# The exact-maxima path of a fused attention and FFN block as a second pass behind the last store, and two jobs of the FFN moved

## The chip, the cores and the metric

One core of a Trainium2 chip runs the whole kernel. The metric is the device time in microseconds (us), taken as the median of repeated runs; a profiled execution beside them gives the trace. PE is the matrix engine (PEld its weight loads), ACT the scalar engine, DVE the vector engine, POOL GpSimd, SP the engine that issues the DMAs.

## The reference

A pre-norm transformer block without biases, in float32, on 2048 tokens of width 576. There are 32 query heads of 18, one shared key head and one shared value head, and a bilinear FFN of width 4608.

```python
h  = x + attention(layernorm(x))           # q = x@wq, k = x@wk, v = x@wv, softmax(q k^T / sqrt(18)) v @ wo
h2 = h + ((layernorm(h) @ w_gate) * (layernorm(h) @ w_up)) @ w_down
```

## The kernel before

**Blocks and pairs.** The tokens are worked on in four blocks of 512. The unit of attention is a *pair* (`pair`, `scores`, `values`): one tile of 128 keys against 512 queries of two heads. PE multiplies (L498) into a PSUM tile `s`, of which there are two, ACT takes the exponential of 128x1024 elements into `P` (L499), and PE later multiplies `P` with the values into `acc` (L503), which is done by `flush`. Eight groups of four heads, 16 key tiles and two pairs for each make 256 pairs per block, 1024 in all. Queries of block 0 run by themselves at the start, first beside the projection of the queries, then alone (`steps`). All other pairs are put between the matmuls of the FFN of earlier blocks.

**The guard.** The softmax subtracts an upper bound of the maxima, worked out from the absolute queries, in place of the maxima. `flag` compares the largest bound with a limit, and `guard` (L384 to L395) branches on the result: with these inputs the bound is below the limit and the branch body is skipped. The body computes the exact maxima (`exact_maxima`) and repeats the seven groups of block 0 that are done by then (`again`, `chunk_of`). It stands in the middle of the attention of block 0, after pair 224. Every engine loads the flag into a register (L387) and branches (L388). A hint for the branch stands at the start of the program for PE, ACT, DVE and SP.

**Projection.** When a group of heads is done, `normalise` and `normal_heads` (L528 to L560) divide by the row sum (`rc`, L544 to L547), transpose, and regroup the rows by DMAs into `ob` (L560). A chunk of `ob` is split into a high and a low part (`chunk`, L563) and multiplied with a chunk of `wo` (`project`, L630). For blocks 1 to 3 `wo`'s chunks are loaded one after the other into one buffer `wor` (`load_wo`, L588), called from `chunk`, and split by POOL and DVE into `wos` (`split_wo`, L88 and L89) in the round after. These jobs wait in a list, and `run_aux` takes one job of it in each *round*; there are two rounds per FFN step (after matmul step 12, and at the end).

**FFN.** Each block has 36 steps of 128 hidden units. A step multiplies `X` with the gate and up weights (L836, 27 pairs of matmuls into `pg` and `pu`, for which there are two PSUM tiles in all), ACT copies one result to `g` (L859), DVE multiplies the other with it to `hf` (L863). Two steps together are multiplied with their part of `w_down` by a scheme of seven products (`down`, L796, 14 stages over three PSUM banks). The results are added to the residual by DVE (L799) or by ACT and POOL (L803, L804). This is done at the end of the next even step. The seven weight combinations are made once, in the FFN of block 0: `right_sums` (L913 to L924) makes three sums on POOL (L915), called at matmul step 16 of the even step; `right` makes the high part on POOL (L939) and the low part on DVE (L942) in the odd step, at matmul steps 7, 9 and so on, and stores them (L945) for the later blocks. `raw` (L911) is the load of the next `w_down` part, issued when `right` ends.

**Order.** The order of instructions on every engine is the order of the calls (a manual schedule). Each engine works its own list strictly in that order and waits on semaphores, so an instruction that waits holds up all that stand behind it on its engine.

At a change of block, `spread` transposes the normalised rows (L679) and splits them into `X`; five chunks are transposed in the order 0 to 4 and taken out of PSUM in the order 4, 0, 2.

Of the kernel before, what the change touches and what calls it, by code (L numbers as in the profile page):

```python
# [17 lines left out]
F32 = mybir.dt.float32  # L18
# [7 lines left out]
P = 128  # L26
# [32 lines left out]
class Block:  # L59
# [312 lines left out]
    def flag(self):  # L372

        dve, lp = self.dve, self.lp
        mx1 = lp.tile([H, 1], F32, tag="mx1", bufs=1, name="mx1")
        dve.tensor_reduce(mx1, self.mx[:, 0:self.n_mx], AX.X, ALU.max)
        psx = self.ps_m("psx")
        self.pe.transpose(psx[0:1, 0:H], mx1, self.ident[:H, :H])
        mx2 = lp.tile([1, 1], F32, tag="mx2", bufs=1, name="mx2")
        dve.tensor_reduce(mx2, psx[0:1, 0:H], AX.X, ALU.max)  # L380
        self.above = lp.tile([1, 1], I32, tag="flag", bufs=1, name="flag")
        dve.tensor_scalar(self.above, mx2, GUARD / SCALE, None, ALU.is_gt)

    def guard(self):  # L384

        self.tc.mark_branch_hint_location("guard", "LikelyTaken", [getattr(mybir.EngineType, e) for e in ("PE", "Activation", "DVE", "SP")])
        fv = self.nc.values_load(self.above, min_val=0, max_val=1, skip_runtime_bounds_check_because="a comparison")  # L387
        with self.tc.If(fv > 0, label="guard"):  # L388
# [8 lines left out]
    def again(self, g):  # L397

        q = self.pp.tile([P, 2, TB], F32R, tag="P", name=f"qa{g}")
        self.load_q(q, 0, g)  # L400
        self.load_m(q, 0, g)
        acc = self.ps_a(f"acca{g}")
        for t in range(NT):
            Ps = []
            for pr in range(2):
                s_ = self.ps_s(f"sa{g}_{t}_{pr}")
                p_ = self.pp.tile([P, 2, TB], F32, tag="P", name=f"Pa{g}_{t}_{pr}")
                self.scores(s_, p_, q, t, pr)
                Ps.append(p_)
            self.values(acc, Ps, t)  # L410
            del Ps, p_, s_
        os_ = self.os.get(g)
        if os_ is None:
            os_ = self.pp.tile([P, TB], F32, tag="P", name=f"osa{g}")
        self.dve.transpose(os_, acc)
        if g not in self.os:
            self.normal_heads(0, g, os_)

    def load_q(self, q, b, g):
        for i, o in enumerate((0, 64)):  # L420
# [107 lines left out]
    def normalise(self, b, g, os_):  # L528
        if g == 0:
            self.ob = self.op.tile([P, 5, TB], F32, tag="ob", name=f"ob{b}")  # L530
        self.normal_heads(b, g, os_)
        del self.os[g]
        c = ({1: 0, 3: 1, 5: 2, 6: 3, 7: 4} if b == 0 else {1: 0, 3: 1, 5: 2, 7: 3}).get(g)
        if c is not None:
            self.aux.append((self.round + (LANDING if b == 0 and c < 4 else 0), lambda: self.chunk(b, c), None))

    def normal_heads(self, b, g, os_):


        dve, ob = self.dve, self.ob  # L540
        o = os_.rearrange("p (k c) -> p k c", c=32)
        rc = self.op.tile([P, TB // 32], F32, tag="rc", bufs=2, name=f"rc{b}_{g}")
        if b == 0:
            dve.tensor_scalar(rc, o[:, :, 0], 1e-30, None, ALU.max)  # L544
            dve.reciprocal(rc, rc)
        else:
            dve.reciprocal(rc, o[:, :, 0])  # L547
        dve.tensor_tensor(o[:, :, 1:1 + DH], o[:, :, 1:1 + DH],
                          rc.unsqueeze(2).broadcast_to([P, TB // 32, DH]), ALU.mult)
        turned = ob[:, 4 if b == 0 or g < NG - 1 else 0]  # L550
        dve.transpose(turned, os_)
        if b == 0 and g == NG - 1:
            return
        for j in range(4):
            r, end, m = DH * (4 * g + j), DH * (4 * g + j + 1), rows(b, 0)
            p = 32 * j + 1
            while r < end:
                c, n = r // m, min(end, (r // m + 1) * m) - r
                for q in (r % m, 64 + r % m)[:1 if c < 4 else 2]:
                    self.sp.dma_start(ob[q:q + n, c], turned[p:p + n])  # L560
                r, p = r + n, p + n

    def chunk(self, b, c):  # L563
# [102 lines left out]
    def spread(self, b):  # L666
# [49 lines left out]

    def more_wd(self, b, n):

        if b:
            self.load_wd(self.n_wd + n)  # L720

    def left_first(self, n, hf):
# [93 lines left out]
    def ffn(self, b):  # L816
        pe, act, dve = self.pe, self.act, self.dve
        X, hid, todo = self.X, [], None
        for f in range(NF):
# [11 lines left out]
            for c in range(9):  # L831
                for wk, xk in ((0, 0), (0, 1), (1, 0)):
# [41 lines left out]
            todo = (f // 2,) if k else None  # L874
        if b + 1 < NB:
            both(self.spread(b + 1), self.down(b, *todo))
            self.more_wd(b + 1, WD_BUFS if b == 0 else 4)
            if b + 2 < NB:
                self.load_x(b + 2)
        else:  # L880
# [45 lines left out]
    def right(self, p):  # L926
# [21 lines left out]
        self.src = None  # L948
        self.load_raw(p + 1)

    def run(self):
# [4 lines left out]
        self.wd_list = [(b, p, j) for b in range(1, NB) for p in range(NC) for j in (range(4) if p == NC - 1 else ORDER)]  # L956
        self.n_wd = 0
        self.m_dram = tc.dram_tile([NB, 2, H, TB], F32, name="m_dram")
        self.known, self.n_mx, self.os, self.chunks = [0] * NB, 0, {}, []
        self.h, self.qt, self.normed, self.wr, self.ws, self.wdo, self.wo_r, self.wos = {}, {}, {}, {}, {}, {}, {}, {}  # L960
        self.n_pair, self.half, self.pend, self.aux, self.round = 0, [], [], [], 0
        self.tqs = []
        self.p2, self.p_next, self.wo_from, self.due = None, -1, 10 ** 6, 0.0
        with ExitStack() as st:
            pool = lambda name, bufs, **k: st.enter_context(tc.tile_pool(name=name, bufs=bufs, **k))
            cp, self.lp, self.hp = pool("const", 1), pool("ln", 2), pool("resid", 2)
# [9 lines left out]
            with tc.tile_pool(name="p0q", bufs=1) as self.p0q:  # L976
# [3 lines left out]
                with tc.tile_pool(name="qb", bufs=2) as self.qb:  # L980
# [7 lines left out]
                    while live:  # L988
# [18 lines left out]
            self.cast = self.act.copy  # L1007
            self.load_w(0)
            self.load_w(1)
            self.fill(2.0, 1)  # L1010
            while 0 not in self.normed:
                self.run_aux(1)
                self.fill(1.0, 1)
            self.split_w(0)
            while self.n_pair % 8 != 4:
                self.pair()
                if not self.half:
                    self.flush(len(self.pend) - 1)
            self.flush(len(self.pend))
            self.normal(0)  # L1020
            for _ in range(2):
                self.pair()
            for i, _ in enumerate(self.spread(0)):
                if i % 2 == 0:
                    self.pair()
            self.flush(len(self.pend))
            del self.oT
            self.room()
            self.load_raw(0)
            for b in range(NB):  # L1030
                self.ffn(b)


RATE = 3.0
# [130 lines left out]
```

## Time and profile before

| | us |
|---|---|
| median of 3 runs | 2355.78 |
| the runs | 2352.33, 2355.87, 2355.78 |
| the profiled execution, its time | 2353.41 |
| the profiled execution, its span | 2351.6 |
| PE busy | 2294.3 |
| ACT busy | 1431.7 |
| DVE busy | 1184.3 |
| POOL busy | 673.8 |
| mean granted PE clock | 0.993 of full speed |

The span runs from the first to the last instruction of the trace; the time of that execution is 1.8 us more. Busy time of PE includes the time in which a pipelined matmul runs under the next. Times in the views are counted from the start of the span.

### The profile page before, as it was taken

The numbers are of one execution on the slowest core, as the hardware profiler recorded it, in microseconds if no ns is written. First come the engines' busy times: TensorE is split into PE (matmuls) and PEld (weight loads), VectorE is DVE, ScalarE is ACT, GpSimd is POOL, SyncE is SP. The second block draws the span as 40 slices with busy tenths as digits, with TensorE's granted clock in tenths as the row PEclk, the third lists the DMA queues.
The fourth block names the chain that finished last, engine by engine and source line by source line (L and its number), as shares of the span: only waits on it lengthen the run. The fifth ranks groups of instructions, "written<-read, shape, count | busy, mean of one in ns | idle before, by whom it ended". The sixth has DMA issues, their size and how long they took to land.

```text
span 2351.6 us, 46322 instructions
## 1 busy us (share of the span) xinstructions
PE 2294.3 (98%) x18225; PEld 1611.6 (69%) x18225; DVE 1184.3 (50%) x2151; ACT 1431.7 (61%) x1868; POOL 673.8 (29%) x873
## 2 busy tenths in 40 slices
PE   5999999999999999999999999999999999999999
PEld 4334434677776767777777667766777778888888
DVE  7333334565555556444444445544444476565665
ACT  4788877766676666567676767567676623232322
POOL 3100000455454444222222212312222224343333
PEclk9999999999999999999999999999999999999999
DMA  4222222444333443633433333544333335655443
GB/s 142 69 65 84 71 80 69 148 147 141 128 125 123 139 149 134 201 117 122 127 122 117 121 100 122 153 156 127 112 121 120 113 129 190 197 188 185 168 167 126
DMA packets 127218, 306.52 MB, mean 130 GB/s; under 512 B 15679, under 2 KB 16447, under 8 KB 126999
## 3 DMA queue, kind: packets, MB, share of 16 engines
q1 hardware_dynamic: 126999, 303.54, 39.6%
q8 instruction: 145, 2.38, 0.4%
q14 instruction: 74, 0.61, 0.1%
HBM read 234.00 MB, written 55.67 MB: 123 GB/s over the span
## 4 chain that ended last, share of the span: by engine, by line
PE 79%; issue 3%; DVE 2%; POOL 1%; ACT 1%; DMA 0%; SPq 0%; DVEq 0%; POOLq 0%; ACTq 0%
PE y L796 17%; PE pg L836 14%; PE acc L503 14%; PE gu L836 12%; PE pu L836 9%; PE s L498 9%; PE yo L630 3%; PE y L754 1%; ACT P L499 1%; POOL x L804 0%; POOL ws L88 0%; PE ye L754 0%; DVE hf L863 0%; DMA X<-X 0%; DVE bsb L103 0%
## 5 line engine op out<-in xcount | busy, mean ns | idle before, releaser
L499 ACT ACTIVATE P<-s 128x1024 f32<-128x1024 f32 x1024 | 1025.3, 1027 | 311.8 <-PE s L498 232.4
L836 PE MATMUL pg<-X,ws 64*128 64x512 f32 x2565 | 699.5, 391 | 0.0
L836 PE MATMUL pu<-X,ws 64*128 64x512 f32 x2565 | 699.2, 391 | 0.0
L836 PEld LDWEIGHTS pg<-X,ws 64*128 64x128 f32 x2565 | 476.5, 186 | 56.2 <-DMA wr<-in_wgu_dram 0.8
L836 PEld LDWEIGHTS pu<-X,ws 64*128 64x128 f32 x2565 | 473.9, 186 | 37.1 <-DVE h L631 0.3
L503 PE MATMUL acc<-P,V 128*32 128x512 f32 x4096 | 492.2, 600 | 0.9 <-ACT P L499 0.6
L498 PE MATMUL s<-q,kT 56*128 56x512 f32 x2048 | 439.1, 423 | 7.0 <-ACT P L499 3.9
L796 PEld LDWEIGHTS y<-wdo,room 128*128 128x128 f32 x2856 | 389.3, 189 | 61.7 <-issue 46.9
L796 PE MATMUL y<-wdo,room 128*128 128x288 f32 x2856 | 410.9, 302 | 10.2 <-DVE hf L863 5.2
L803 ACT COPY tmp<-y 128x288 f32<-128x288 f32 x408 | 162.5, 399 | 341.2 <-PE y L796 326.1
L498 PEld LDWEIGHTS s<-q,kT 56*128 56x128 f32 x2048 | 195.9, 185 | 208.6 <-ACT P L499 119.4
L836 PE MATMUL gu<-X,ws 64*128 64x512 f32 x2646 | 308.1, 389 | 0.3 <-DMA X<-X 0.2
L836 PEld LDWEIGHTS gu<-X,ws 64*128 64x128 f32 x2646 | 258.0, 184 | 43.9 <-issue 3.8
L503 PEld LDWEIGHTS acc<-P,V 128*32 128x32 f32 x4096 | 114.8, 109 | 250.3 <-issue 232.5
L804 POOL TENSOR_TENSOR x<-x,tmp 128x288 f32<-128x288 f32 x204 | 159.2, 811 | 411.9 <-ACT tmp L803 410.5
L88 POOL CAST ws<-wr 128x1152 fp32r<-128x1152 f32 x144 | 168.4, 1170 | 322.8 <-PE gu L836 102.4
L804 POOL TENSOR_TENSOR h<-h,tmp 128x288 f32<-128x288 f32 x204 | 159.5, 810 | 327.0 <-ACT tmp L803 326.5
L89 DVE TENSOR_TENSOR ws<-wr,ws 128x1152 fp32r<-128x1152 f32 x144 | 196.7, 1366 | 75.2 <-POOL ws L88 75.2
L863 DVE TENSOR_TENSOR hf<-pu,g 128x512 f32<-128x512 f32 x95 | 65.5, 689 | 258.2 <-ACT g L859 258.1
L799 DVE TENSOR_TENSOR x<-x,y 128x288 f32<-128x288 f32 x272 | 117.1, 452 | 143.4 <-PE y L796 143.4
L799 DVE TENSOR_TENSOR h<-h,y 128x288 f32<-128x288 f32 x272 | 117.2, 453 | 95.4 <-PE y L796 92.6
L89 DVE TENSOR_TENSOR room<-S,room 128x1024 fp32r<-128x1024 f32 x68 | 83.3, 1225 | 152.9 <-ACT room L88 152.9
(170 smaller groups left out, 1716.9 us busy)
## 6 DMA issues: line engine op xcount, KB each, us to landing
wdo<-wd_dram SPq DMA_DIRECT2D x369, 288.0 KB
wr<-in_wgu_dram SPq DMA_DIRECT2D x144, 576.0 KB
wd_dram<-wdo SPq DMA_DIRECT2D x123, 288.0 KB
q<-q_dram SPq DMA_DIRECT2D x64, 216.0 KB
raw<-in_wd_dram SPq DMA_DIRECT2D x36, 288.0 KB
q_dram<-qs SPq DMA_DIRECT2D x16, 504.0 KB
X<-X SPq DMA_DIRECT2D x28, 256.0 KB
x<-in_x_dram SPq DMA_DIRECT2D x16, 288.0 KB
```

What stands on the lines that cost most here:

```text
L88: (copy or self.cast)(hi, src)
L89: self.dve.tensor_tensor(lo, src, f32(hi), ALU.subtract)
L498: self.pe.matmul(s_[:, i], self.kT[o:o + 56, t * P:(t + 1) * P], q[o:o + 56, pr], start=True, stop=True)
L499: self.act.activation(p_, s_, AF.Exp, scale=SCALE)
L503: self.pe.matmul(acc[32 * j:32 * j + 32, :], self.V[:, t, :], Ps[j // 2][:, j % 2, :], start=(t == 0), stop=(t == NT - 1), skip_group_chec ...
L630: pe.matmul(y[:, :HD], m, k, start=(i == 0), stop=(i == len(ms) - 1))
L796: pe.matmul(y[:, :HD], m[:, t * P:(t + 1) * P], k, start=(first and j == 0), stop=(j == 2), skip_group_check=True)
L799: dve.tensor_tensor(hs, hs, y[:, :HD], ALU.add)
L803: act.copy(z, y[:, :HD])
L804: pool.tensor_tensor(hs, hs, z, ALU.add)
L836: pe.matmul(ps, w[o:o + 64, wk, c], X[o:o + 64, xk, c], start=(j == 0), stop=(j == 26))
L863: dve.tensor_tensor(hf, pu, g, ALU.mult)
```

## The change

Five things are edited.

1. The guard moves behind the last store of the whole program. Its body is now a complete second pass: exact maxima, then attention and FFN of all blocks again (`begin(False)`, `blocks`). The hint is dropped. `again` goes, and the list of chunks with it. POOL now has work in the body too. To serve both passes, the code from the load of the first `wo` on is put into `blocks`.
2. With that the pairs of block 0 run on without the flush at pair 224: `load_wo_0` is split over the steps up to pair 228, the flag is worked out in the steps up to pair 236, and the projections of block 0 may begin at pair 240 instead of 236.
3. `right_sums` is called at matmul step 4 of the odd step, no longer at step 16 of the even one.
4. `load_wo` of chunks 0 to 3 is called from `normalise`, ahead of the DMAs of `ob`; chunk 4's stays in `chunk`. `split_wo` waits one round more after the load.
5. `normal_heads` bounds the row sum from below in all blocks, not in block 0 alone (one more DVE instruction on 128x16 per group), and `spread` transposes chunk 4 first in blocks 1 to 3.

```diff
     def guard(self):
-        self.tc.mark_branch_hint_location("guard", "LikelyTaken", [getattr(mybir.EngineType, e) for e in ("PE", "Activation", "DVE", "SP")])
         fv = self.nc.values_load(self.above, min_val=0, max_val=1, skip_runtime_bounds_check_because="a comparison")
         with self.tc.If(fv > 0, label="guard"):
             self.exact_maxima()
-            for g in range(self.n_pair // (2 * NT)):
-                self.again(g)
-            for c in self.chunks:
-                self.chunk_of(0, c)
-            for (b, g), q in self.qt.items():
-                self.load_m(q, b, g)
+            self.begin(False)
+            self.known = [H] * NB
+            self.prefetch_q(0, 0)
+            self.load_x(0)
+            self.load_x(1)
+            self.blocks()
...
     def normalise(self, b, g, os_):
...
+        c = ({1: 0, 3: 1, 5: 2, 6: 3, 7: 4} if b == 0 else {1: 0, 3: 1, 5: 2, 7: 3}).get(g)
+        if b and c is not None:
+            self.load_wo(c)
         self.normal_heads(b, g, os_)
         del self.os[g]
-        c = ({1: 0, 3: 1, 5: 2, 6: 3, 7: 4} if b == 0 else {1: 0, 3: 1, 5: 2, 7: 3}).get(g)
...
-        if b == 0:
-            dve.tensor_scalar(rc, o[:, :, 0], 1e-30, None, ALU.max)
-            dve.reciprocal(rc, rc)
-        else:
-            dve.reciprocal(rc, o[:, :, 0])
+        dve.tensor_scalar(rc, o[:, :, 0], 1e-30, None, ALU.max)
+        dve.reciprocal(rc, rc)
...
     def chunk(self, b, c):
...
-        if b == 0:
-            self.chunks.append(c)
-        else:
+        if b and c == 4:
             self.load_wo(c)
...
-        if self.wo_r and not self.wos and self.wo_round < self.round:
+        if self.wo_r and not self.wos and self.wo_round + 1 < self.round:
...
-        for c, n, t in sorted(tx, key=lambda x: x[0]):
+        for c, n, t in tx:
...
-                    if b == 0 and j == 16 and not k:
-                        self.right_sums(f // 2)
-                        parts = self.right(f // 2)
-                    if b == 0 and k and j > 6 and j % 2:
-                        next(parts, None)
+                    if b == 0 and k and self.first:
+                        if j == 4:
+                            self.right_sums(f // 2)
+                            parts = self.right(f // 2)
+                        elif j > 6 and j % 2:
+                            next(parts, None)
...
+    def blocks(self):
+
+        work = self.load_wo_0()
+        self.steps(lambda: self.n_pair < WO_FROM, work)
+        drain(work)
+        self.wo_from = WO_FROM + 12
+        if self.first:
+            work = self.flag()
+            self.steps(lambda: self.n_pair < WO_FROM + 8, work)
+            drain(work)
+        self.cast = self.dve.tensor_copy
+        self.steps(lambda: self.more(0))
+        self.cast = self.act.copy
...
+        for b in range(NB):
+            self.ffn(b)
...
     def run(self):
...
-            self.flag()
             self.wp, self.hh, self.p2 = pool("w", 2), pool("hid", 4), pool("P2", 1)
-            wo_parts = self.load_wo_0()
-            self.steps(lambda: self.n_pair % (2 * NT), wo_parts)
-            self.flush(len(self.pend))
+            self.blocks()
             self.guard()
-            self.wo_from = self.n_pair + 12
-            self.steps(lambda: self.more(0), wo_parts)
-            drain(wo_parts)
...
+WO_FROM = 228
```

`flag` gets a `yield` after its first instruction, so that its PE transpose comes one step later. The rest of the moved code, from the first load of gate weights to the FFN loop, is the same in `blocks` as it was in `run`.

More of the change, by code (lines that the diff above doesn't have):

```diff
@@ L717, in more_wd @@
     def more_wd(self, b, n):
-        if b:
+        if b or not self.first:
             self.load_wd(self.n_wd + n)
@@ L876, in ffn @@
             both(self.spread(b + 1), self.down(b, *todo))
-            self.more_wd(b + 1, WD_BUFS if b == 0 else 4)
+            self.more_wd(b + 1, WD_BUFS if b == 0 and self.first else 4)
             if b + 2 < NB:
@@ L949, in right, with begin @@
         self.load_raw(p + 1)
+    def begin(self, first):
+        self.first = first
+        self.wd_list = [(b, p, j) for b in range(first, NB) for p in range(NC) for j in (range(4) if p == NC - 1 else ORDER)]
+        self.n_wd = 0
+        self.os, self.h, self.qt, self.normed, self.wr, self.ws, self.wdo, self.wo_r, self.wos = ({} for _ in range(9))
+        self.n_pair, self.half, self.pend, self.aux, self.round = 0, [], [], [], 0
+        self.p_next, self.wo_from, self.due = -1, 10 ** 6, 0.0
+    def blocks(self):
[10 more added lines that the diff above has]
+        self.cast = self.act.copy
+        self.load_w(0)
+        self.load_w(1)
+        self.fill(2.0, 1)
+        while 0 not in self.normed:
+            self.run_aux(1)
+            self.fill(1.0, 1)
+        self.split_w(0)
+        while self.n_pair % 8 != 4:
+            self.pair()
+            if not self.half:
+                self.flush(len(self.pend) - 1)
+        self.flush(len(self.pend))
+        self.normal(0)
+        for _ in range(2):
+            self.pair()
+        for i, _ in enumerate(self.spread(0)):
+            if i % 2 == 0:
+                self.pair()
+        self.flush(len(self.pend))
+        del self.oT
+        self.room()
+        if self.first:
+            self.load_raw(0)
+        else:
+            self.load_wd(WD_BUFS)
+        for b in range(NB):
+            self.ffn(b)
+        del self.A, self.o_hl, self.S, self.tmp, self.X, self.ob, self.mv
     def run(self):
@@ L955, in run @@
         self.wd_dram = tc.dram_tile([NC, P, 7, 2, HD], F32, name="wd_dram")
-        self.wd_list = [(b, p, j) for b in range(1, NB) for p in range(NC) for j in (range(4) if p == NC - 1 else ORDER)]
-        self.n_wd = 0
         self.m_dram = tc.dram_tile([NB, 2, H, TB], F32, name="m_dram")
[L959 to L963, printed above, removed]
+        self.known, self.n_mx = [0] * NB, 0
+        self.tqs, self.p2 = [], None
+        self.begin(True)
         with ExitStack() as st:
@@ L997, in run @@
                         self.flush(len(self.pend) - 1)
-            self.flag()
             self.wp, self.hh, self.p2 = pool("w", 2), pool("hid", 4), pool("P2", 1)
-            wo_parts = self.load_wo_0()
-            self.steps(lambda: self.n_pair % (2 * NT), wo_parts)
-            self.flush(len(self.pend))
+            self.blocks()
             self.guard()
-            self.wo_from = self.n_pair + 12
-            self.steps(lambda: self.more(0), wo_parts)
-            drain(wo_parts)
[L1007 to L1031, printed above, removed]
 RATE = 3.0
```

21 lines of the change are left out of this document (1 added, 20 removed).

## The prediction

> **What bounds the kernel now.** I read the page's busy times first, then PE's rows with an idle time before them, then what ended those waits, then the granted clock of the stretches behind them.
>
> ```profile
> PE 2294.3 (98%) x18225; PEld 1611.6 (69%) x18225; DVE 1184.3 (50%) x2151; ACT 1431.7 (61%) x1868; POOL 673.8 (29%) x873
> ```
>
> PE is busy for 2294.3 of 2351.6 us, so nearly everything beside PE is hidden, and an edit that leaves PE's work alone can gain only where PE stands still (57 us in all) or runs slowly. Behind the start, which the change doesn't touch, two kinds of place stand out. The first is the guard:
>
> ```profile
> 323.24 0.73 PE L498 MATMUL s<-q,kT 56*128 56x512 f32 x4 [2.38 <-SPq L388]
> 315.99 3.77 ACT L499 ACTIVATE P<-s 128x1024 f32<-128x1024 f32 x4 [1.43 <-PE s L498]
> 323.83 3.85 ACT L499 ACTIVATE P<-s 128x1024 f32<-128x1024 f32 x4 [4.07 <-PE s L498]
> 329.25 1.94 ACT L499 ACTIVATE P<-s 128x1024 f32<-128x1024 f32 x2 [1.57 <-PE s L498]
> 332.26 3.77 ACT L499 ACTIVATE P<-s 128x1024 f32<-128x1024 f32 x4 [1.07 <-PE s L498]
> 325.40:332.20 6.80, 6.38 (x28) 1.69 (x26) 2.73 (x5) 4.22 (x5) 0.00 (x0) 0.50 0.35 90
> ```
>
> In these rows come start, duration, engine and line; in brackets the idle time before and what ended it. Here attention runs alone, and ACT sets the pace: 3.77 us for four exponentials, 0.943 us each. At the branch PE waits 2.38 us for SP's branch (L388) and ACT loses 4.07 us. The last row is a stretch of time with each engine's busy time; its third figure from the end is the granted clock of PE: 0.50. The trace shows half speed right behind the stall, and ACT loses 1.57 and 1.07 us more to it.
>
> The second kind is in the FFN, six times:
>
> ```profile
> PE y L796 <- DVE hf L863: 5.2, 4, 3.1
> 878.84 1.54 PE L796 MATMUL y<-wdo,room 128*128 128x288 f32 x5 [3.06 <-DVE hf L863]
> 1393.15 1.13 PE L630 MATMUL yo<-wos,room 128*128 128x288 f32 x5 [1.90 <-DVE h L631]
> 1891.54 1.87 PE L796 MATMUL y<-wdo,room 128*128 128x288 f32 x8 [3.58 <-DVE h L799]
> 870.92 0.43 SPq L588 DMA_DIRECT2D wor<-in_wo_dram  x1
> 876.06 0.67 POOL L88 CAST wos<-wor 128x576 fp32r<-128x576 f32 x1 [15.85 <-DMA wor<-in_wo_dram]
> 876.76 1.33 DVE L89 TENSOR_TENSOR wos<-wor,wos 128x576 fp32r<-128x576 f32 x1 [7.87 <-POOL wos L88]
> POOL wos L88 <- DMA wor<-in_wo_dram: 103.3, 13, 15.8
> ```
>
> The first of these rows is from the view of waits: 5.2 us in 4 waits, the longest 3.1, which is the next row; the other three are near 503, 627 and 752. PE names DVE, but at 876 DVE itself stood idle for 7.87 us: its next instruction, the low part of `wos`, waited for POOL's high part, and that for the load of `wo`, which SP had issued 5.1 us before. The last row, from the view of waits too, says that POOL meets 13 loads like this.
>
> **Part 1, the guard leaves the attention.** From 315.99 to 332.26 ACT does 10 exponentials in 16.27 us; at 0.943 they take 9.43, so 6.84 go. Ahead of it 1.43 us of idle time become the usual 0.2 or so, since the transpose of the flag now comes a step after the reduction it waits for. Together **-8.0**. What is late next is the end of block 0's chain: its projections start 4 pairs later, while the FFN begins at the same pair.
>
> ```profile
> 379.09 0.37 PE L630 MATMUL yo<-wo,oT 128*128 128x288 f32 x1 [0.55 <-ACT oT L88]
> 384.14 0.66 PE L630 MATMUL yo<-wo,oT 128*128 128x288 f32 x3 [0.58 <-DVE x L631]
> 391.30 1.70 POOL L663 COPY xh<-xh 128x64 f32<-128x64 f32 x4 [53.88 <-DVE xh L662]
> 396.69 2.40 PE L679 MATMUL tx<-C,xh 128*128 128x128 f32 x20 [0.95 <-ACT P L499]
> ```
>
> From the last projection (384.80) the normalised rows take until 393.00, 8.2 us; today 10 pairs cover this, 10.9 us of PE; in the new order 7 pairs remain, some 7.7 us and the wait of 0.95. That just holds. Chunk 3's high part moves to ACT, behind exponentials, where chunk 4's already costs 0.55. I charge **+0.7** (0 to 3).
>
> **Part 2, wo's loads.** Chunks 0 to 3 are loaded a round earlier, ahead of `ob`'s DMAs and what follows them in SP's queue.
>
> ```profile
> 857.33 6.73 SPq L560 DMA_DIRECT2D ob<-ob  x9
> 1879.25 6.89 SPq L560 DMA_DIRECT2D ob<-ob  x9
> 1886.18 0.47 SPq L588 DMA_DIRECT2D wor<-in_wo_dram  x1
> ```
>
> At 870.92 the load moves to about 857, at 1886.18 to about 1879: 7 to 13 us earlier, against the 5.1 us to its landing. The split stays in the round that it has now, because the extra round of waiting balances the earlier load; so DVE finds its data there. All six stalls belong to chunks 0 to 3. Their gaps sum to 5.2 + 1.90 + 3.58 = 10.7 us. Three of them are followed by half speed:
>
> ```profile
> 878.30:881.70 3.40, 2.86 (x12) 2.89 (x13) 1.58 (x4) 0.67 (x2) 2.00 (x3) 0.50 0.00 0
> 1393.70:1397.10 3.40, 3.40 (x15) 3.12 (x16) 2.33 (x7) 0.00 (x0) 0.00 (x0) 0.51 0.00 0
> 1892.10:1895.50 3.40, 3.40 (x16) 3.40 (x16) 0.83 (x2) 1.19 (x3) 1.94 (x3) 0.50 0.32 89
> 1885.65 1.35 DVE L89 TENSOR_TENSOR ws<-wr,ws 128x1152 fp32r<-128x1152 f32 x1
> ```
>
> Each 3.4 us at 0.50 loses 1.7, together 5.1. At 1888 a rest stays: `ws` ends at 1887.0, the low part of `wos` (1.33) still stands before the residual adds, so PE resumes near 1888.85 and not at 1887.96: 0.9. Sum **-14.9** (-5 to -16). The Trainium skill's page "TensorE: Matmul & The Clock Gate", section "What's actually happening", says that the clock is halved after about one idle window of 3.4 us; by that rule gaps of 1.90 and 3.06 us would be too short, the 5.1 would not be there, and the sum would end 5.1 us higher. The trace disagrees: 0.51 behind the gap of 1.90. Each load costs SP 0.43 us ahead of `ob`'s DMAs, which are used a round later and have that time.
>
> **Part 3, the right sums.** Three POOL instructions move from a step in which POOL has time to the odd step of block 0, ahead of the casts that feed DVE, with `hf` behind them in DVE's queue, and PE's next step needs the PSUM tile that `hf` reads. Two such steps, without and with a group's normalisation in them:
>
> ```profile
> L915 POOL TENSOR_TENSOR sums<-raw,sums x17: 799/809/1191, 411.8 to 903.5; 128x288 f32<-128x288 f32 x17
> 454.33 0.66 POOL L939 CAST wdo<-raw 128x288 fp32r<-128x288 f32 x1
> 459.36 0.50 PE L498 MATMUL s<-q,kT 56*128 56x512 f32 x2
> 484.57 0.65 POOL L939 CAST wdo<-raw 128x288 fp32r<-128x288 f32 x1
> 485.82 1.39 DVE L942 TENSOR_TENSOR wdo<-raw,wdo 128x288 fp32r<-128x288 f32 x1
> 487.13 0.68 DVE L863 TENSOR_TENSOR hf<-pu,g 128x512 f32<-128x512 f32 x1
> 489.38 0.50 PE L498 MATMUL s<-q,kT 56*128 56x512 f32 x2
> ```
>
> Three sums of 0.81 put POOL's last cast 2.43 us later: 457.4 and 487.65. DVE's last low part then runs beside POOL's next cast, as it does at 485.82, and takes 1.39: 458.8 and 489.05. `hf` ends at 459.5 and 489.75. PE needs its tile 0.33 us after the quoted pair: 459.7 and 489.7. So nothing to 0.1 in the 9 plain steps, 0.1 to 0.4 in the 8 others: 9 x 0.05 + 8 x 0.25 = **+2.5** (0 to 32, below).
>
> **Part 4, the branch at the end.** SP is last there.
>
> ```profile
> 2345.13 3.51 SPq L788 DMA_DIRECT2D out_dram<-h  x4
> L1161 SPq DRAIN  x3: 7/7/13, 2350.7 to 2351.1; - x3
> L387 SPq TENSOR_LOAD <-flag x1: 494/494/494, 317.9 to 317.9; - x1
> L388 SPq COMPARE_BRANCH x1: 70/70/70, 318.4 to 318.4; - x1
> L388 PEldq COMPARE_BRANCH x1: 397/397/397, 320.4 to 320.4; - x1
> ```
>
> SP's last store is issued by 2348.64; its landing is awaited until 2350.7. Now 0.49 and 0.07 us stand between, then a jump over a long body without a hint, which no row shows: below, the hinted jump of PE, whose next event comes at 320.9 and so at once; above, the 5.1 us of a load. I take the store's own 2.0, being one transfer's way: 2351.2, and 0.5 for the semaphores of the branch not taken: **+1.2** (0 to 4.3). The other engines do this before SP.
>
> **Part 5, the small ones.**
>
> ```profile
> L544 DVE TENSOR_SCALAR rc<-os x8: 155/168/633, 101.4 to 372.4; 128x16 f32<-128x16 f32 x8
> 2006.13 1.53 PE L679 MATMUL tx<-C,xh 128*128 128x128 f32 x12 [0.43 <-DVE hf L863]
> ```
>
> I take them at nothing. The bound on the row sum is 24 more DVE instructions of 0.17 us, hidden under a busy PE like the rest of the normalisation; where that cover is gone, in the 8 tight steps above, it costs up to 8 x 0.17 = 1.4. With chunk 4 transposed first, PE has four transposes more to do during the wait of 0.43 at 2006, but needs POOL's copies first, four in 1.70 us (391.30): -0.4 to +0.4 for each of three changes of block.
>
> **Sum.** -8.0 + 0.7 - 14.9 + 2.5 + 1.2 = -18.5. The profiled execution took 2353.4, so 2334.9; the median shown is 2.4 above it: **2337**.
>
> **Rivals.** (a) POOL's sums meet the low part of `ws` on DVE and only the first is slowed to 1.19: 0.4 more in each of 17 steps, 2344. (b) The stall at 320.87 isn't the branch but the wait for `wo`'s first load, which SP issues at the same point as before; then Part 1 stays: 2345. Against it: PE's row names SP's branch. (c) The loads of `wo` land no earlier, because their buffer or SP's queue holds them: only -3.6 remains, 2352. Against it: the buffer is free rounds before. (d) **Slower:** the sums stand in line with DVE's two-input instructions, `ws` (1.35) and `room` (0.64), one by one. Then POOL is not 2.43 but 4.4 us late, `hf` ends near 461.5 and 491.7, PE waits 1.8 to 2.0 in 17 steps, 32 us; the sum becomes +11: 2367, and more if these gaps halve the clock as that of 1.90 did. It decides from 1.24 us per step (21 us over 17), where the gains are used up. For it speaks the 1.39 beside a POOL cast; against it, the cast at 454.33, which runs among DVE's low parts and takes 0.66. The Trainium skill's page "SBUF — State Buffer", section "SBUF: two separate sides", calls the port pair shared by DVE and GpSimd an exclusive lock, held for a whole instruction; that rule leads to (d).
>
> **How the numbers follow.** Forecast 0.70 (2329 to 2343), (a) 0.10, (b) 0.05, (c) 0.08, (d) 0.07. The range 2328 to 2350 holds the first three, 0.85. A measurement here tells 0.2% (4.7 us) from no change: faster 0.85, same 0.08 from (c), slower 0.07 from (d).
>
> **What would show it.** Right: ACT's exponentials at 0.94 us without a break near 320; no wait of POOL's `wos` for `wor` in chunks 0 to 3; PE's clock at 1 near 878, 1393 and 1892; `hf` of the odd steps close to PE's next step. Wrong: waits of PE for `hf` (L863 before) in every odd step of block 0, a new gap before `tx`, or more than 5 us between the last store and the end.

## The result

The changed kernel takes 2346.45 us (median of 6 runs, 2345.44 to 2346.81), the kernel before in the runs beside it 2355.49. The ratio is 0.9964 (95% interval 0.9951 to 0.9977): 9.0 us faster, where I had forecast 18.8 (2355.78 less 2337). In a second set of runs it was 2345.63 beside 2353.97, ratio 0.9965 (0.9951 to 0.9979). The sign and the wide range (2328 to 2350) held; the forecast's own band (2329 to 2343) did not, and the size was half of what I had said. One run of the first experiment (3169.74 us) and one of the second (5651.60 us) lie far above all others, and the medians and ratios below are those of the other runs.

The profiled execution took 2345.53, 7.9 less than that of before, and so did its span (2343.7 against 2351.6). First its busy row, then two of PE's rows in the view of waits (engine, line, what it waited for; us in total, times, longest):

```profile
PE 2292.6 (98%) x18225; PEld 1605.7 (69%) x18225; DVE 1207.9 (52%) x2174; ACT 1431.9 (61%) x1869; POOL 673.1 (29%) x873
```

```profile
PE pu L811 <- DVE hf L839: 4.1, 7, 0.8
PE psx L379 <- DVE mx L376: 2.3, 1, 2.3
```

The four waits for `hf` of the kernel before (5.2 us in all) and PE's wait for SP's branch (2.4) are gone, but two rows have taken their place: seven waits of `pu` for `hf`, and one of the flag's transpose for the flag's own reduction. DVE's busy time rose from 1184.3 to 1207.9 us, though it has only 23 more instructions: some instructions on DVE got longer.

Where the time went can be read without a guess, because PE executes the same 18225 matmuls in both. I took the ends of the same matmuls in PE's order, named the stretches between them by the times of the changed kernel, and compared their lengths:

```
stretch (us)                  before   after   difference   forecast
300 to 403, guard             105.03  102.99      -2.0        -7.3
480 to 900, block 0           419.11  419.99      +0.9        -4.4
1380 to 1420                   43.85   40.12      -3.7        -3.6
1875 to 1925                   53.77   49.97      -3.8        -4.4
1990 to 2040                   51.23   49.81      -1.4         0
behind PE's last matmul         4.10    6.51      +2.4        +1.2
the rest                                          -0.2         0
all                          2351.53 2343.68      -7.9       -18.5
```

(The second row's forecast is 2.5 for the right sums less 6.9 for the four loads in block 0. The first difference holds both terms of Part 1. The last row counts to the start of the last event, 0.05 us before the end of the span.) Two rows carry the miss: the guard by 5.3 us, block 0 by 5.3.

**The guard.** PE, then ACT, then DVE in the timeline of the changed kernel (start, duration, engine and line; in brackets the idle time before and its cause), and two rows of the view by stretches (the third figure from the end is the granted clock of PE):

```profile
325.62 1.07 PE L481 MATMUL acc<-P,V 128*32 128x512 f32 x8
328.99 0.20 PE L379 MATMUL psx<-C,mx 32*1 32x32 f32 x1 [2.30 <-DVE mx L376]
```

```profile
323.21 3.79 ACT L477 ACTIVATE P<-s 128x1024 f32<-128x1024 f32 x4 [0.24 <-PE s L476]
330.02 1.94 ACT L477 ACTIVATE P<-s 128x1024 f32<-128x1024 f32 x2 [3.03 <-PE s L476]
333.04 1.94 ACT L477 ACTIVATE P<-s 128x1024 f32<-128x1024 f32 x2 [1.08 <-PE s L476]
```

```profile
322.03 5.26 DVE L89 TENSOR_TENSOR wo<-wo_r,wo 128x576 fp32r<-128x576 f32 x5 [0.76 <-POOL wo L88]
...
328.83 0.10 DVE L376 TENSOR_REDUCE mx<-mx 32x1 f32<-32x8 f32 x1
```

```profile
329.00:332.40 3.40, 3.40 (x15) 1.03 (x17) 0.32 (x2) 1.94 (x2) 0.00 (x0) 0.50 0.15 37
331.70:335.10 3.40, 3.40 (x16) 0.70 (x12) 0.00 (x0) 2.20 (x3) 0.00 (x0) 0.50 0.66 188
```

The stall at the branch is gone, but a stall of nearly the same length stands 6 us later: PE waits 2.30 us, and the clock behind it is 0.50 again. What it waits for lasts 0.10 us. It is late because of its place in DVE's queue: `blocks` drains `load_wo_0` before it starts `flag`, so the reduction stands behind five low parts of `wo` (5.26 us) and group 6's normalisation.

How long the clock stays at 0.50 differs between executions of the same code. Here it is 6.8 us (328.3 to 335.1). In the second profiled execution of the changed kernel (the fifth experiment below) PE's gap is 2.11 us and the half clock ends after 3.4 us, at 333.7; the gap and the next 3.4 us there are:

```profile
330.21 0.18 PE L379 MATMUL psx<-C,mx 32*1 32x32 f32 x1 [2.11 <-DVE mx L376]
333.70:337.10 3.40, 2.98 (x24) 0.80 (x22) 0.00 (x0) 2.98 (x4) 0.00 (x0) 0.99 0.85 243
```

So the guard's difference to the kernel before is -2.0 us in the one and -3.2 in the other. Of the eight profiled executions with this order, three have 6.8 us of half clock (the stretch 300 to 347 takes 46.8 to 47.1) and five 3.4 us (45.5 to 45.9). What decides between the two, no run shows.

**Block 0.** POOL, then DVE and in the last two rows PE, around the end of an odd step at 488, one of the steps with a normalisation in them:

```profile
477.28 0.82 POOL L891 TENSOR_TENSOR sums<-raw 128x288 f32<-128x288 f32 x1
478.18 1.80 POOL L891 TENSOR_TENSOR sums<-raw,sums 128x288 f32<-128x288 f32 x1
479.95 0.99 POOL L891 TENSOR_TENSOR raw<-raw,raw 128x288 f32<-128x288 f32 x1
480.88 0.43 POOL L915 CAST wdo<-raw 128x288 fp32r<-128x288 f32 x1
```

```profile
477.36 1.96 DVE L89 TENSOR_TENSOR ws<-wr,ws 128x1152 fp32r<-128x1152 f32 x1 [1.27 <-POOL ws L88]
479.24 1.03 DVE L89 TENSOR_TENSOR room<-hf,room 128x256 fp32r<-128x256 f32 x1
481.34 0.65 DVE L918 TENSOR_TENSOR wdo<-raw,wdo 128x288 fp32r<-128x288 f32 x1 [1.07 <-POOL wdo L915]
...
482.51 0.39 DVE L523 TENSOR_SCALAR rc<-os 128x16 f32<-128x16 f32 x1
...
485.00 1.38 DVE L918 TENSOR_TENSOR wdo<-sums,wdo 128x288 fp32r<-128x288 f32 x1
...
488.24 0.67 DVE L839 TENSOR_TENSOR hf<-pu,g 128x512 f32<-128x512 f32 x1
487.77 0.40 PE L811 MATMUL pg<-X,ws 64*128 64x512 f32 x1
488.97 0.50 PE L811 MATMUL pu<-X,ws 64*128 64x512 f32 x1 [0.80 <-DVE hf L839]
```

The three sums take 3.61 us here and not the 2.43 that I had charged: the second takes 1.80 beside the low part of `ws`, which itself takes 1.96 in place of 1.35. DVE then waits 1.07 us for POOL's first cast. From there DVE has no more idle time: two low parts, the normalisation (2.5 us), five low parts, `hf`. PE waits 0.80 us for it.

Not every odd step is like this one. In 11 of the 17 the second sum meets the low part of `ws` and the three take 3.6 to 3.7 us. In the other six they take 2.4 to 2.5 us, in five of them beside residual adds on DVE, which have one of their two inputs in PSUM; there `hf` ends some 2.5 us before PE's next step, as in the kernel before. Of the 11 steps the seven with a normalisation wait; the four without one keep 0.12 to 0.17 us.

**What held.** The places of the former stalls, in the changed kernel: three rows by stretches with their granted clock, PE's row of what is left at 1884, and SP's row of the load that stood behind the largest stall of block 0:

```profile
878.30:881.70 3.40, 3.40 (x26) 3.29 (x26) 1.30 (x3) 1.53 (x4) 1.55 (x2) 1.00 0.77 287
1386.00:1396.00 10.00, 10.00 (x84) 7.22 (x78) 7.00 (x15) 4.74 (x6) 0.01 (x1) 1.00 0.13 32
1881.00:1895.00 14.00, 13.23 (x98) 11.61 (x96) 11.66 (x23) 3.90 (x9) 5.76 (x7) 1.00 0.59 197
1884.00 2.27 PE L771 MATMUL y<-wdo,room 128*128 128x288 f32 x15 [0.61 <-DVE h L774]
859.58 0.43 SPq L563 DMA_DIRECT2D wor<-in_wo_dram  x1
```

The clock is 1.00 in all three. Of POOL's 13 waits for `wor` (103.3 us) one of 0.8 us is left. The load that SP issued at 870.92 now goes out at 859.58; counted by the same matmul of PE that is 857.8 in the kernel before, 13.1 us earlier.

### The profile page after: what moved, and what is told of

It is laid out like the page before. It is cut to its first block, busy times and chain, and to the rows that moved or that the text cites. A ratio compares the mean times of both kernels' runs of the same rounds, so it can differ in the third digit from the quotient of the medians.

```text
span 2343.7 us, 46343 instructions
## 1 busy us (share of the span) xinstructions
PE 2292.6 (98%) x18225; PEld 1605.7 (69%) x18225; DVE 1207.9 (52%) x2174; ACT 1431.9 (61%) x1869; POOL 673.1 (29%) x873
## 4 chain that ended last, share of the span: by engine, by line
PE 88%; DVE 4%; POOL 3%; issue 2%; ACT 1%; DMA 1%; SPq 0%; POOLq 0%; ACTq 0%; DVEq 0%
PE acc L481 19%; PE y L771 16%; PE pg L811 13%; PE s L476 12%; PE gu L811 12%; PE pu L811 10%; PE yo L605 3%; PE psq L331 3%; POOL wdo L915 1%; DVE wdo L918 1%; PE y L729 1%; ACT P L477 1%; POOL ws L88 0%; POOL x L779 0%; DVE hf L839 0%
## 5 line engine op out<-in xcount | busy, mean ns | idle before, releaser
L89 DVE TENSOR_TENSOR ws<-wr,ws 128x1152 fp32r<-128x1152 f32 x144 | 204.2, 1418 | 77.5 <-POOL ws L88 77.5
```

The costliest lines, as they stand in the source:

```text
L89: self.dve.tensor_tensor(lo, src, f32(hi), ALU.subtract)
```

## The experiments

All but the fifth and the seventh edit the changed kernel. They were run in three sets on three chips: the first four, the next four, and the last two. The ratio is that to the kernel before in the same set; only the second set has the changed kernel beside it as well. The kernel before differs by up to 0.15% between sets (2352.12 to 2355.49), and it was 3.4 us faster beside the first four than beside the changed kernel, so that a time there that meets an expectation worked out from 2346.45 shows little by itself. Set against the changed kernel's 0.9964, the ratios of the first four and the last two have intervals that overlap with its own. So small differences are read from the stretches of the traces, one profiled execution each; the length of a stretch without an edit agrees to 0.1 us between runs in most places. The first 62 us (61.6 to 64.0), the 238 us behind them and the 455 from 1420 on (1 us each) and the guard's stretch with its half clock (45.5 to 47.1, as above) vary more. The seven short stretches in which `pu` waits for `hf` are 480 to 500, 548 to 562, 608 to 625, 673 to 690, 734 to 757, 800 to 815 and 860 to 900.

### The flag's reduction ahead of wo's splits

```diff
-        work = self.load_wo_0()
+        fl = self.flag() if self.first else None
+        if fl:
+            next(fl)
+        work = self.load_wo_0()
...
-            work = self.flag()
-            self.steps(lambda: self.n_pair < WO_FROM + 8, work)
-            drain(work)
+            self.steps(lambda: self.n_pair < WO_FROM + 8, fl)
+            drain(fl)
```

> The changed kernel (2346.45) with one edit: the flag's first reduction is issued ahead of wo's splits instead of behind them; its transpose stays where it is. Theory (the branch's stall came back as a wait for this 0.10 us reduction, which stands in DVE's queue behind five low parts of wo, 5.26 us, and a normalisation): PE's gap of 2.30 us ahead of psx at 328.99 and the half clock behind it go; ACT's 4 exponentials between 326.99 and 335.76, 8.77 us, take some 4.1: -4.7, so 2341.8 (2340.5 to 2343). Rival (the pace here is set by something else that is only hidden by this wait, wo's split or the projections behind it): a gap opens at 330 to 345 instead, at most -2: 2344.5 or more. The original sum's -8.0 would be reached if -5.9 came: 2340.5.

2342.20, ratio to before 0.9956 (0.9943 to 0.9969). DVE, PE and ACT:

```profile
315.55 0.15 DVE L376 TENSOR_REDUCE mx<-mx 32x1 f32<-32x8 f32 x1
324.75 0.18 PE L379 MATMUL psx<-C,mx 32*1 32x32 f32 x1
323.51 11.94 ACT L477 ACTIVATE P<-s 128x1024 f32<-128x1024 f32 x12 [0.24 <-PE s L476]
```

The transpose has no wait in front of it, and ACT runs twelve exponentials without a break (11.94 / 12 = 0.995 each). No half clock is left near the guard. The stretch 300 to 347 falls from 47.06 to 42.55, by 4.5, or by 3.3 from the 45.87 of the second profiled execution of the changed kernel; there is no new gap behind it (347 to 403: 55.93 and 55.94). The order in DVE's queue was the cause. With it 300 to 403 is 98.49, 6.5 less than before, where my sum had 7.3.

### The right sums back in the even step

```diff
-                    if b == 0 and k and self.first:
-                        if j == 4:
-                            self.right_sums(f // 2)
-                            parts = self.right(f // 2)
-                        elif j > 6 and j % 2:
-                            next(parts, None)
+                    if b == 0 and self.first and j == 16 and not k:
+                        self.right_sums(f // 2)
+                        parts = self.right(f // 2)
+                    if b == 0 and self.first and k and j > 6 and j % 2:
+                        next(parts, None)
```

> The changed kernel (2346.45) with one edit: the right sums go back to the even step, j = 16. Theory (the sums make hf late in the odd steps with a group's normalisation): the seven waits of pu for hf and what follows each (0.73 to 1.45 us, 8.1 in all by the drift against the kernel before) go: 2338.4 (2337 to 2340). Rival (the waits come from the normalisation, with its added bound on the row sum and wo's loads ahead of it, and not from the sums): waits of pu for hf stay, -2 at most: 2344.5 or more.

2338.67, ratio 0.9944 (0.9931 to 0.9957). No wait of PE for `hf` is left between 403 and 960. The seven short stretches lose 1.40, 0.72, 1.38, 0.78, 1.37, 0.78 and 1.42: 7.85. By the ratios the edit is worth 4.7 us, with 3 us to either side for each of the two ratios. The same step as above, in this kernel's times:

```profile
475.95 0.44 POOL L914 CAST wdo<-raw 128x288 fp32r<-128x288 f32 x1
479.28 0.39 DVE L523 TENSOR_SCALAR rc<-os 128x16 f32<-128x16 f32 x1
484.16 0.68 DVE L838 TENSOR_TENSOR hf<-pu,g 128x512 f32<-128x512 f32 x1
486.46 0.39 PE L811 MATMUL pg<-X,ws 64*128 64x512 f32 x1
486.46 0.40 PE L811 MATMUL pu<-X,ws 64*128 64x512 f32 x1
```

`hf` ends at 484.84, 1.6 us before PE needs its tile. The normalisation with the added instruction is in this step too; without the sums it costs nothing here.

### Without the bound on the row sum

```diff
-        dve.tensor_scalar(rc, o[:, :, 0], 1e-30, None, ALU.max)
-        dve.reciprocal(rc, rc)
+        dve.reciprocal(rc, o[:, :, 0])
```

> The changed kernel (2346.45) without the bound on the row sum in normal_heads: one DVE instruction of 0.16 to 0.39 us less for each group, in all blocks. Left out: the maximum with 1e-30 in all blocks. Theory A (in the seven odd steps with a normalisation DVE's queue sets when hf ends, low parts standing behind the normalisation): each of the 7 steps gains 0.2 to 0.4: 2344.4 (2343.5 to 2345.2). Theory B (POOL's late casts set it, DVE waits for them): no change, 2346.4 (2346 to 2347).

2343.00, ratio 0.9959 (0.9946 to 0.9972). PE's waits for `hf` in block 0:

```profile
PE pu L810 <- DVE hf L838: 1.7, 4, 0.4
```

Each of the seven stretches is 0.32 to 0.41 shorter, 2.5 in all: PE gains nearly all of the 0.39 us that DVE saves ahead of `hf`. That is Theory A. The time lies below what either theory had; the stretches decide. The span fell by 2.1; the guard's stretch was 1.5 shorter as well, with 3.4 us of half clock in place of 6.8.

### The branch hint

```diff
     def guard(self):
+        self.tc.mark_branch_hint_location("guard", "LikelyTaken", [... PE, Activation, DVE, SP])
         fv = self.nc.values_load(self.above, ...)
```

> The changed kernel (2346.45) with the branch hint of the kernel before put back, for the branch at the end. Theory (the 2.7 us between SP's branch at 2339.1 and its next event at 2341.8 are the jump over the long body without a hint; with a hint the engines of the kernel before needed 0.1 to 1.95 us): -0.8 to -2.0, so 2345.0 (2344.4 to 2345.7); the last store's landing, some 2 us after its issue, then ends last. Rival (the jump costs the same, since its target has to be fetched either way): 2346.4.

2345.18, ratio 0.9970 (0.9958 to 0.9981). The branch (COMPARE_BRANCH) and the first event behind it (EVENT_SEMAPHORE) in the changed kernel, then with the hint; behind the colon durations, then first and last start:

```profile
L388 DVEq COMPARE_BRANCH  x1: 72/72/72, 2338.1 to 2338.1; - x1
L388 DVEq EVENT_SEMAPHORE  x1: 21/21/21, 2341.3 to 2341.3; - x1
L388 SPq COMPARE_BRANCH  x1: 50/50/50, 2339.1 to 2339.1; - x1
L388 SPq EVENT_SEMAPHORE  x8: 17/17/17, 2341.8 to 2342.4; - x8
```

```profile
L389 DVEq COMPARE_BRANCH  x1: 84/84/84, 2338.4 to 2338.4; - x1
L389 DVEq EVENT_SEMAPHORE  x1: 21/21/21, 2339.0 to 2339.0; - x1
L389 SPq COMPARE_BRANCH  x1: 70/70/70, 2339.5 to 2339.5; - x1
L389 SPq EVENT_SEMAPHORE  x8: 17/17/17, 2340.7 to 2342.2; - x8
```

Without the hint ACT, DVE and SP come back 2.6 to 3.2 us after their branch and PE 4.2, before SP has done so. With it ACT and DVE need 0.5 to 0.6 and PE 1.9, but SP, which is last, 1.2, and its eight semaphores then take 1.5 in place of 0.6. The tail falls only from 6.51 to 6.03, less than the 0.8 that I had expected at least. The time lies where I had expected it, but its ratio is no better than the changed kernel's, so the time doesn't show the gain. In the sixth experiment, with the same hint, SP comes back after 0.9, its semaphores take 1.2 and the tail falls by 1.2. So the hint takes 0.5 to 1.2 us off the tail, and at least half of the 2.4 us that the branch costs there stays.

### The changed kernel once more

> The changed kernel itself, unchanged, as the measure for the runs beside it on the same chip. Before took 2355.49 in one set of runs and 2352.12 in another, so the sets differ by 0.14%. If the change is worth the 0.36% of the first set here too: 9.0 below before; by the single runs of the first experiments 7 to 10 below.

2345.63 beside 2353.97: 8.3 less, as expected. It serves as the measure for the sixth to the eighth experiment.

### Three edits together

The edits of the first, second and fourth experiment in one kernel.

> The changed kernel with the flag's reduction ahead of wo's splits, the right sums back in the even step and the hint at the branch. Theory (three causes in three stretches that don't touch each other): the savings that the traces showed in the stretches add up: 4.5 (300 to 347), 7.9 (the seven stretches around 480 to 900) and 0.5 (behind PE's end): 12.9 below the changed kernel beside it, 2333.5 if that takes 2346.4. Rival (the three share a cover, as the odd steps' slack: part is counted twice): 8 to 11 below the changed kernel beside it, 2335.5 to 2338.5.

2334.09, 11.5 below the changed kernel beside it, ratio to before 0.9913 (0.9898 to 0.9928). By time this lies between the two expectations; the stretches decide. 300 to 347 is 42.55 again, the seven stretches of block 0 are 8.1 shorter, and behind PE's last matmul it takes 5.30 in place of 6.49: 3.3 (against 45.87 in the run beside it) or 4.5 (against 47.06), 8.1 and 1.2. In the stretches the savings add up. What hides part of them in the time is the guard's stretch, which was 1.2 shorter in the second run of the changed kernel (3.4 us of half clock in place of 6.8), and the first 62 us, which were 1.2 longer in this one. This version is faster than both kernels.

### Wo's loads alone, in the kernel before

```diff
     def normalise(self, b, g, os_):
...
+        if b and c is not None:
+            self.load_wo(c)
         self.normal_heads(b, g, os_)
...
-        else:
+        elif c == 4:
             self.load_wo(c)
...
-        if self.wo_r and not self.wos and self.wo_round < self.round:
+        if self.wo_r and not self.wos and self.wo_round + 1 < self.round:
```

> The kernel before with one part of the change: wo's loads of chunks 0 to 3 a round earlier, the split where it was. Theory (the loads were the cause of all six stalls in the FFN, and this part is worth what I had summed): 14.9 below the kernel before, by stretches 7.4 in block 0, 3.7 at 1391 and 3.8 at 1888: 2340.6 if that takes 2355.5. Rival (the stalls in block 0 went because the right sums left the even step, which gave POOL and DVE time there, so the loads alone are worth less): only the two behind block 0 go, 7.5 below: 2348.0.

2339.60, 14.4 below the kernel before; ratio 0.9937 (0.9923 to 0.9950). By stretches 7.2 in block 0 (0.79, 1.09, 0.85 and 4.45), 3.74 at 1391 and 3.76 at 1888: 14.7. I had summed 14.9. By time this one part is worth more than the whole change.

### Without the branch at the end

```diff
             self.blocks()
-            self.guard()
```

> The changed kernel without the branch at the end and without the second pass behind it (left out: the check of the flag and the exact path, which these inputs don't take). Theory: the time from PE's end to the end of the span falls from 6.5 to the 4.1 of the kernel before: 2.4 below the changed kernel beside it, 2344.0 if that takes 2346.4. Rival (the long body behind the branch also costs on the way, by code that is fetched in between): more than 4 below.

2343.86, 1.8 below the changed kernel beside it; ratio 0.9955 (0.9941 to 0.9968). Behind PE's last matmul 3.98 us in place of 6.49: -2.5. By the stretches the code of the second pass costs nothing on the way.

### Two sums in place of three

```diff
         sub(s[4], s[6], s[1])
-        sub(s[5], s[3], s[4])
+        s[5] = s[4]
         sub(s[6], s[3], s[6])
```

> The changed kernel without the second of the three right sums (left out: that sum; the products that use it take the first one). Two sums, one of them beside the low part of ws, take 0.81 + 1.80 = 2.6 us, about the 2.43 that I had charged for three. Theory (my step was right in how POOL's lateness reaches PE, and wrong in the duration: three sums take 3.6): with 2.6 PE hardly waits for hf, the seven stretches around 480 to 900 lose at least 6 of their 7.9: 2338.5 to 2340 if the changed kernel takes 2345.6. Rival (sums of any length in the odd step push DVE's low parts behind the normalisation, that is, the low parts' order costs it): less than 3 of it goes: 2343 or more.

2342.04, ratio 0.9946 (0.9928 to 0.9964). The sums, in ns (least, median, most), in the changed kernel and here:

```profile
L891 POOL TENSOR_TENSOR sums<-raw x17: 792/812/843, 414.0 to 919.5; 128x288 f32<-128x288 f32 x17
L891 POOL TENSOR_TENSOR sums<-raw,sums x17: 796/1803/1811, 414.9 to 920.4; 128x288 f32<-128x288 f32 x17
L891 POOL TENSOR_TENSOR raw<-raw,raw x17: 797/987/1001, 415.6 to 921.1; 128x288 f32<-128x288 f32 x17
```

```profile
L891 POOL TENSOR_TENSOR raw<-raw,raw x17: 797/1803/1811, 414.2 to 916.4; 128x288 f32<-128x288 f32 x17
```

Whichever sum meets the low part of `ws` takes 1.80: before it was the second, now it is the third. The seven stretches are 4.68 longer than with the sums in the even step, against 7.85 with three sums. So neither theory holds whole. Two sums take 2.6 us, 0.2 more than the delay that I had charged, and still cost 4.7 us: 0.67 for each of the seven steps and not my 0.25. The third sum adds the other 3.2.

### The old order of the transposes

```diff
-        for c, n, t in tx:
+        for c, n, t in sorted(tx, key=lambda x: x[0]):
```

> The changed kernel with the transposes at a change of block in the old order, chunk 4 last. Theory (the order is what shortens the stretch 1990 to 2040 by 1.4 us, by two waits of PE, 0.43 for hf's PSUM tile and 0.60 for DVE's X): both waits come back, 1.4 more in that stretch, nothing at the other two changes of block: 2347.0 if the changed kernel takes 2345.6. Rival (it was the earlier loads of wo): the stretch stays at 49.8 and the time as it is.

2347.17, ratio 0.9968 (0.9956 to 0.9981). Here, then in the changed kernel:

```profile
1998.72 1.53 PE L654 MATMUL tx<-C,xh 128*128 128x128 f32 x12 [0.44 <-DVE hf L839]
...
2001.65 1.62 PE L729 MATMUL y<-wdo,room 128*128 128x288 f32 x10 [0.60 <-DVE X L661]
```

```profile
1996.26 2.62 PE L654 MATMUL tx<-C,xh 128*128 128x128 f32 x20
1998.63 3.64 PE L729 MATMUL y<-wdo,room 128*128 128x288 f32 x23
```

Both waits are back, and 1990 to 2040 takes 50.91 in place of 49.81: 1.1 more, and nothing at the other two changes of block. The order is the cause of that 1.1; the other 0.3 of the 1.4 in the table stays open.

## Why the prediction was half right

The direction was right, and so was the largest term. Two steps failed, one in Part 1 and one in Part 3, and they make up nearly all of the missing 10 us. 2346.45 lies nearer to the times of rivals (a) and (b), 2344 and 2345, than to my 2337.

**Part 2, wo's loads (-14.9): right.** Alone they give 14.4 by time and 14.7 by stretches: 7.2 in block 0 for my 6.9, 3.7 at 1391 for my 3.6, 3.8 at 1888 for my 4.4. The three half-clock stretches go with gaps of 1.90 to 3.58 us, as the sum had it. At 1888 I had left a rest of 0.9; 0.61 stayed. In the sentence on the idle window of 3.4 us I let all 5.1 us go; the gap of 3.58 us is longer than that window, so only the 3.4 us behind the two shorter gaps would have gone. Nothing else in the sum hangs on it.

**Part 1, the guard (-7.3, measured -2.0 and -3.2): the step that failed is "Ahead of it 1.43 us of idle time become the usual 0.2 or so, since the transpose of the flag now comes a step after the reduction it waits for".** It counts the steps between the reduction and its reader on PE, and not what stands ahead of the reduction on DVE: 5.26 us of low parts and a normalisation. So a wait of 2.30 us came in place of the one of 2.38, and with the half clock behind it took back 4.5 us of the gain, or 3.3 where the half clock was short. The first experiment shows it: with the reduction ahead of the low parts, 300 to 347 is 6.5 shorter than before, for my 8.0, and the +0.7 behind it does not appear (55.97 before, 55.94). Rival (b) had the time near (2345) by luck: its mechanism, a wait for `wo`'s first load, is not what the rows show.

**Part 3, the right sums (+2.5, measured +7.9): mis-sized, in three terms.** That nothing would happen in the plain steps was right, with 0.12 to 0.17 us to spare in four of them. Of the eight steps for which I took 0.25, seven wait, and they lose 1.1 each. First, the sums take 3.6 us there, not 2.43: 3.2 of the 7.9. Second, I let POOL's last cast set `hf`. By the third experiment it is DVE: POOL's first cast comes late, and from there the low parts stand behind the normalisation without a gap, so that 0.39 us less there is 0.35 us less on PE. So a delay close to the one that I had charged costs 4.7. Third, the bound on the row sum, which I had put at up to 1.4 where cover is gone and charged at nothing, is worth 2.5 in these seven steps; it is a part of the 7.9, and how large it is with two sums no run shows.

**Rivals (a) and (d).** Sums and DVE's two-input instructions do hold each other up, as (d) said: between 477.28 and 480.94 the reported ends are those of `sums`, `ws`, `sums`, `room`, `sums` (478.10, 479.32, 479.98, 480.27, 480.94), in turn. In this order the rows agree with the exclusive lock of the Trainium skill's page "SBUF — State Buffer", section "SBUF: two separate sides", which I had given too little weight. In the price they do not wholly: behind 478.10 the last four take 2.84 us, while their times elsewhere (1.35, 0.81, 0.64 and 0.81) add up to 3.61. So where (d) failed was the price: POOL is 3.6 us late and not 4.4, that is 1.2 us more than I had charged and not 2.0; and in six of the seventeen steps the sums meet no low part of `ws`, in four more there is just slack enough. Against the price of (a), 0.4 in every step, it is more per step and in fewer steps.

**Part 4, the end (+1.2, measured +2.4): within its bounds.** My terms add up to +1.0 and not to +1.2: SP's first DRAIN at 2351.7 where it was at 2350.7. Behind the end of the last store, the load and the branch took 0.7 us for my 0.56, the jump 2.7 for 2.0, and the semaphores 0.6 for the 0.5 that I had read from no row. Another 0.5 then passes until SP's first DRAIN (2342.9), which I had not counted. SP's own hinted branch in the kernel before (318.4, next event at 320.4) had already taken 2.0 us; I had set the lower bound by PE's.

**Part 5 (0, measured -1.4 and, within Part 3, +2.5).** At the change of block I counted the first wait (0.43) and not the second (0.60): with chunk 4 first DVE also has its part of X earlier. The experiment puts the order at 1.1.

## What to carry to other kernels

Where an instruction is moved, its place in the queue of its own engine decides when it ends: list what is issued ahead of it there, however short it is itself. Where two engines feed a third, find the one without idle time in the steps that matter: there nearly every added part of a microsecond counts (0.35 of 0.39 here), and an average cover says nothing. And look, for each part of a change, at the place where it pays: here one part earned 14.4 us, one cost 7.9 and one failed to earn 3.3 to 4.5, and two small edits restore both.

## What the runs showed of the hardware

- A POOL sum of 0.81 us took 1.80 beside the low part of `ws`, a DVE instruction with two inputs, and that one 1.96 in place of 1.35. The sum before it, `ws` and this sum took 2.70 together (477.28 to 479.98), where their single times add up to 2.97. Beside residual adds on DVE, which have two inputs too, but one of them in PSUM, the same sum took 0.81 (at 509.5). POOL's casts in the same steps took 0.43 and 0.53 us in the median, 1.6 at most.
- A wait of PE cost more than its idle time. At 488 `pu` starts 1.20 us after its `pg`, while in the second experiment both start together. Only 0.80 of this is idle time in the trace, since `pg` runs for the first 0.40. The first matmuls behind it take 0.50 for 0.39, and the stretch is 1.40 longer. With two sums no such wait above 0.2 us stands in the list, and the stretches are still 0.6 to 0.75 longer.
- Gaps of PE of 1.90 to 3.58 us were followed by a granted clock of 0.50 for 3.4 or 6.8 us, and gaps of nearly the same length by either (2.11 by 3.4, 2.30 by 6.8). Behind the longest gap between 340 and 2340 in the changed kernel, 1.24 us at 1929, it stayed at 1.00.
- From its branch over the long body to its next event an engine without a hint took 2.6 to 3.2 us, PE 4.2. With a hint it was 0.5 to 0.6 on ACT and DVE, 1.9 on PE, and 0.9 to 1.2 on SP.
